# Kernel taps at half-step offsets, tap products for four channel groups in one matmul, all first loads in one ring, engine lists ordered anew

## The chip, the cores and the metric

The kernel runs on one core of one Trainium2 chip. The metric is the device time of one execution in microseconds (us). Each kernel is run several times. A run is called slow here when it is over 1.5% above the fastest run of the same kernel on that chip, otherwise fast. Ratios and comparisons below are of fast runs unless a sentence says otherwise; the median that is quoted first for a run is of all its runs, slow ones too. A profile is one further execution, seen by the hardware profiler; its span is 1.5 to 2.9 us shorter than that execution's measured time.

Engine names in the profile: PE is the matmul engine, PEld its weight loads, DVE the vector engine, ACT the scalar engine, POOL and SP two further queues.

## The reference

```python
def reference(A_u, ...):
    xn = _layernorm(A_u)                       # [1, 2048, 512]
    # branch A: S4 state space layer: a long convolution along the 2048 positions, by FFT
    logdA, dB = dt * A, dt * Bc                # 512 channels x 128 modes, complex
    P = jnp.exp(logdA[:, :, None] * l)         # l = 0..2047
    K = jnp.einsum("dn,dnl,dn->dl", Cc, P, dB).real
    s = irfft(rfft(pad(xn)) * rfft(pad(K)))[:2048] + xn * Dskip
    # branch B: the one row with the largest xn @ w_r goes through a gated expert (F = 1376)
    g = silu(xn + scatter(expert(xn[row])))
    return A_u + s * g
```

(Padding, casts and helper functions are left out.) The kernel does the convolution in the frequency domain: the spectrum of `xn` by two DFT passes (`f1`, `f2`), and the spectrum of the filter `K` by a trick: `K` is sampled at a few positions around 20 centres ("taps"), and a fixed matrix `W` turns these samples into the spectrum.

## The kernel before

Everything is recorded into a list of operations with their read and write footprints; a fixed list for each engine says in which order it issues them, and semaphores are set from the footprints. So nearly all matmuls have one source line (the helper's), and groups are told apart by the names of their tiles: `PB<-GG,QQ` are the tap products, `PB<-KT,CA` the transposes behind them, `PB<-KT,W` the filter's spectrum, `PB<-XN,CB` and `PB<-BT,F2T` the two DFT passes, `PB<-PAB,FA` the way back, `PB<-CA,AD` the arguments of the exponentials.

The part that changes most, the samples of `K`. Channels come in 4 quarters `q` of 128; each quarter is done in two chunks (`js`), 8 chunks in all. A chunk is 64 channels: 4 groups `gp` of 16 (`jj`). For every channel the product over the 128 modes of `QQ` (32 positions) and `GG` (20 centres), real and imaginary part (`ci`), is one 32-column matmul of 20 moving columns:

```python
def kgen(c):
    q, js = c // 2, c % 2
    qb = c % 2
    mms = []
    for jj in range(16):
        for ci in range(2):
            for gp in range(4):
                # out: 32 partitions of bank 4; weights 128 x 32; moving 128 x 20
                mms.append((PB[32*gp:32*gp+32, 4, 20*jj:20*jj+20], QQ[:, qb, ci, gp, 0:32, jj],
                            GG[:, 0, ci, :, 32*gp + 16*js + jj], ci == 0, ci == 1))
    kp = KP[:]
    # ... one more pair of matmuls for the sample at position 0 ...
    g.M(mms)                                   # 128 tap matmuls in one go
    act(KT[:, js], PB[:, 4, 0:320].rearrange("p (c t m) -> p m t c", t=5, m=4), ACT.Copy, 320)
    # ... 16 transposes: IDENT (32 columns) x KT[:, js, m, :, :], 80 contiguous columns ...
    act(KT2[:, q, :, 64*js:64*js+64]..., PB[:, 4, 0:320]..., ACT.Copy, 320)
```

`QQ` is laid out `[128, buffer, ci, gp, position, 16 jj]`: the weight columns of one channel are 16 elements (32 bytes) apart. `GG` is `[128, ci, centre, 128 channels]`: the 20 moving columns of one channel are 128 elements (256 bytes) apart. In both layouts the vector engine's operations write whole rows of channels.

The loads and the fillers:

```python
g.dma(SP, [(LD4[:], ...)]); pload("ar"); ca_load = g.dma(SP, [(CA[:], ...)]); ...  # parameters: SP's ring
for q in range(4):
    xl = g.dma(AC, [xsrc[q]])                                 # X in four parts: ACT's ring
# [...]
for k in range(4):                                            # warm-up: 16 matmuls of 128x512
    g.M([(PB[:, 6 + k % 2, :], AT[:, 0, 0:128], warm, True, True) for _ in range(4)])
# [...]
_FILL = [(7, 6, 5), (11, 2, 4), ..., (154, 2, 20)]            # place in PE's list, bank, number of fillers
```

The comments are ours. A ring is the DMA queue of the engine that issues the transfers. The fillers are dense matmuls into free banks (the profile has 47 on their own line, L275); they are meant to hold the matmul engine's clock up where it would wait. `spec(pt)` makes the spectrum in four parts, s0 to s3, each in four steps; a step is 40 matmuls `KT,W`, a copy by ACT, two multiplications by DVE, 32 matmuls `PAB,FA` and a copy by ACT.

## Time and profile before

| what | before |
|---|---|
| time, median of 3 runs | 209.75 us (209.18 to 210.92) |
| profiled span | 206.6 us |
| PE busy, matmuls | 175.7 us, 3170 |
| ACT busy / DVE busy | 136.2 / 142.6 us |
| first bn_stats / first normalized XN / first tap product | 8.8 / 27.7 / 59.1 us |
| second spectrum (s1) starts | 106.3 us |

(bn_stats is the vector engine's first step of the layer norm, XN the normalized input.)

From the page of before: busy time with the share of the span and the number of instructions; the span in 40 slices with tenths of busy time (PE) and of the full matmul clock (PEclk); the instruction queue with packets, MB and share; and the chain of work that ended last.

```profile
PE 175.7 (85%) x3170; PEld 127.9 (62%) x3181; DVE 142.6 (69%) x344; ACT 136.2 (66%) x164; POOL 13.9 (7%) x24
...
PE   6099998889993999967999998999999649999960
...
PEclk9999999995555589985999999889999757999997
...
q8 instruction: 25, 0.41, 0.8%
...
PE 60%; ACT 12%; DVE 10%; issue 8%; DMA 7%; SPq 0%; DVEq 0%
```

The matmul engine is busy nearly throughout, and 60% of the chain lies on it. "issue" is time in which an engine waited for nothing that the profile shows. The clock row is to be read with care at its start: the trace records the clock of before only from 29.8 us on, and the page draws the time before that as full, although 16 `CA,AD` matmuls that take 0.62 us at 100.9 took 1.04 us at 23.7. The groups of instructions of before, by cost: line, engine, operation, tiles, shapes, count | busy us, mean ns of one | idle time before them and what ended it.

```profile
L187 PE MATMUL PB<-KT,W 128*128 128x128 bf16 x640 | 40.1, 224 | 0.7 <-ACT KT L740 0.4
...
L740 ACT ACTIVATE KT<-PB 128x320 bf16<-128x320 f32 x16 | 10.7, 671 | 20.2 <-PE PB L187 20.2
L187 PE MATMUL PB<-GG,QQ 128*32 128x20 bf16 x1024 | 19.8, 223 | 3.9 <-issue 3.9
...
L187 PE MATMUL PB<-BT,F2T 128*64 128x256 bf16 x128 | 11.3, 307 | 1.9 <-issue 1.6
```

The mean of a matmul (223 ns) is its length in the pipeline, not its share of the time: 1024 of them took 19.8 us, 19 ns each. That is why throughput is better read from the timeline, in which successive matmuls of one kind are one row: start, length, what, and in brackets the idle time before it. Before, around the first and the fourth chunk of taps:

```profile
59.06 2.42 PE L187 MATMUL PB<-GG,QQ 128*32 128x20 bf16 x128
61.30 0.27 PE L187 MATMUL PB<-KP,CB 128*4 128x64 bf16 x2
61.49 0.58 PE L187 MATMUL PB<-FT,ERU 128*128 128x1 bf16 x14
65.19 0.75 PE L187 MATMUL PB<-FT,ERU 128*128 128x1 bf16 x19 [3.11 <-issue]
...
87.89 0.33 PE L187 MATMUL PB<-KT,CA 128*32 128x80 bf16 x16
...
91.34 2.25 PE L187 MATMUL PB<-GG,QQ 128*32 128x20 bf16 x118
94.79 0.39 PE L187 MATMUL PB<-GG,QQ 128*32 128x20 bf16 x10 [1.20 <-issue]
```

A chunk of taps takes 2.42 us. Inside runs of one kind of matmul there are five holes that no wait in the profile explains: 3.1 us (above, at 62.1), 1.6, 1.2 (above, at 93.6), 2.1 and 2.7 us, in sum 10.6 us. Counted over all of the trace's records of the matmul engine (matmuls, weight loads, semaphore instructions), they come after instructions 1212, 2235, 2490, 5305 and 5561: multiples of 256 apart, give or take one. The DMA records of the packed trace tie them to the instruction queue: a packet of 16,384 bytes lands in or just before each hole (at 63.6, 88.7, 93.6, 161.3 and 167.5 us), and the hole ends 1.2 to 1.6 us after that landing. (The other 20 packets land without such a hole.)

The table of windows gives, for a stretch of time, busy us and instruction count of PE, PEld, DVE, ACT, POOL, then mean matmul clock, DMA share and GB/s. The stretch from the first tap product to the second spectrum, before:

```profile
59.10:106.30 47.20, 40.71 (x1000) 32.83 (x1001) 26.55 (x61) 29.63 (x38) 3.09 (x5) 0.77 0.56 187
```

### The profile page before, as it was taken

The page shows a single profiled execution, that of the slowest core. Times are in us where ns is not written, and L with a number is a line of the kernel's source. Part 1 is how long each engine was busy: PE and PEld are TensorE (multiplying, and loading weights), DVE is VectorE, ACT ScalarE, POOL GpSimd, SP SyncE. Part 2 cuts the span into 40 slices and gives each one's busy share as a digit, 9 for nine tenths or more (in the row PEclk, how much of TensorE's full clock was granted, in tenths as well). Part 3 has the DMA queues.
Part 4 walks back from the last instruction along what each step waited for, and adds up shares of the span by engine and source line. Part 5 has one row for each costly group of instructions (what it writes and reads, how often), then busy time and mean ns, then how long its engine had stood idle before and what let it go on. Part 6 is the DMA issues. An engine that isn't in the chain of part 4 may idle for free.

```text
span 206.6 us, 7069 instructions
## 1 busy us (share of the span) xinstructions
PE 175.7 (85%) x3170; PEld 127.9 (62%) x3181; DVE 142.6 (69%) x344; ACT 136.2 (66%) x164; POOL 13.9 (7%) x24
## 2 busy tenths in 40 slices
PE   6099998889993999967999998999999649999960
PEld 2044547555883766946898875876799327895420
DVE  1599589997970789801699999959999205542634
ACT  2059589997703978661799999986688422566431
POOL 0074000000000203000000000200002400000000
PEclk9999999995555589985999999889999757999997
DMA  6989972225595692980037297441349852366874
GB/s 176 347 272 405 415 292 84 86 83 156 138 297 185 175 293 51 408 370 8 18 87 205 75 261 198 127 112 33 75 105 306 191 123 51 94 195 178 189 167 102
DMA packets 40528, 36.85 MB, mean 178 GB/s; under 512 B 26577, under 2 KB 35922, under 8 KB 39602
## 3 DMA queue, kind: packets, MB, share of 16 engines
q1 hardware_dynamic: 37458, 20.12, 35.7%
q0 software_dynamic: 2464, 14.19, 19.5%
q10 hardware_dynamic: 576, 2.10, 3.1%
q8 instruction: 25, 0.41, 0.8%
q14 instruction: 5, 0.04, 0.1%
HBM read 25.91 MB, written 10.49 MB: 176 GB/s over the span
## 4 chain that ended last, share of the span: by engine, by line
PE 60%; ACT 12%; DVE 10%; issue 8%; DMA 7%; SPq 0%; DVEq 0%
PE PB L187 58%; DMA STG<-in_A_A_re_dram 3%; ACT U L740 3%; DMA DD<-scr_z 3%; ACT K2T L740 2%; PE PB L275 2%; DVE TT L711 2%; DVE XN L720 2%; ACT QQ L740 2%; ACT ZT L740 1%; DMA scr_z<-ZT 1%; DVE ZB L711 1%; ACT KT L740 1%; ACT XN L740 1%; DVE T L711 1%
## 5 line engine op out<-in xcount | busy, mean ns | idle before, releaser
L187 PE MATMUL PB<-KT,W 128*128 128x128 bf16 x640 | 40.1, 224 | 0.7 <-ACT KT L740 0.4
L187 PEld LDWEIGHTS PB<-KT,W 128*128 128x128 bf16 x640 | 37.3, 100 | 4.2 <-ACT KT L740 1.6
L187 PE MATMUL PB<-CA,AD 32*128 32x256 bf16 (+1 forms) x192 | 24.9, 309 | 5.7 <-DVE AD L724 5.0
L711 DVE TENSOR_TENSOR TT<-GG,ZB 128x512 bf16<-128x512 bf16 (+2 forms) x64 | 27.7, 469 | 0.4
L711 DVE TENSOR_TENSOR PAB<-U,K2T 128x1024 bf16<-128x1024 bf16 x32 | 21.3, 685 | 8.6 <-ACT K2T L740 8.6
L740 ACT ACTIVATE K2T<-PB 128x1024 bf16<-128x1024 f32 x16 | 16.5, 1034 | 14.5 <-PE PB L187 14.4
L187 PEld LDWEIGHTS PB<-CA,AD 32*128 32x128 bf16 x192 | 15.5, 114 | 15.7 <-DVE AD L724 5.9
L711 DVE TENSOR_TENSOR QQ<-QQ,EE 128x2048 bf16<-128x2048 bf16 x16 | 19.5, 1220 | 7.1 <-ACT QQ L740 7.0
L740 ACT ACTIVATE KT<-PB 128x320 bf16<-128x320 f32 x16 | 10.7, 671 | 20.2 <-PE PB L187 20.2
L187 PE MATMUL PB<-GG,QQ 128*32 128x20 bf16 x1024 | 19.8, 223 | 3.9 <-issue 3.9
L187 PEld LDWEIGHTS PB<-GG,QQ 128*32 128x32 bf16 x1024 | 18.8, 170 | 6.3 <-issue 4.3
L187 PE MATMUL PB<-PAB,FA 64*128 64x128 bf16 x512 | 17.9, 222 | 0.6 <-ACT ZT L740 0.4
L740 ACT ACTIVATE U<-PB 128x1024 bf16<-128x1024 f32 x16 | 16.3, 1037 | 2.6 <-PE PB L187 2.6
L740 ACT ACTIVATE ZT<-PB 128x1024 bf16<-128x1024 f32 x16 | 16.5, 1033 | 2.0 <-PE PB L187 2.0
L740 ACT ACTIVATE EE<-PB 128x1024 bf16<-128x1024 f32 x16 | 15.5, 1029 | 2.2 <-PE PB L187 2.2
L187 PEld LDWEIGHTS PB<-PAB,FA 64*128 64x128 bf16 x512 | 15.1, 97 | 3.0 <-ACT ZT L740 0.8
L740 ACT ACTIVATE AT<-PB 128x1024 bf16<-128x1024 f32 x16 | 16.5, 1085 | 0.7 <-PE PB L187 0.7
L711 DVE TENSOR_TENSOR TF<-PB,XN 128x512 bf16<-128x512 f32 x12 | 8.1, 686 | 11.9 <-PE PB L187 8.3
L275 PE MATMUL PB<-CA 128*128 128x512 bf16 x47 | 15.1, 439 | 1.3 <-issue 1.2
L711 DVE TENSOR_TENSOR GG<-TT 128x512 bf16<-128x512 bf16 (+2 forms) x32 | 15.0, 469 | 0.4
L187 PE MATMUL PB<-XN,CB 128*128 128x256 bf16 (+1 forms) x80 | 14.4, 314 | 0.6 <-DVE XN L720 0.5
L187 PE MATMUL PB<-BT,F2T 128*64 128x256 bf16 x128 | 11.3, 307 | 1.9 <-issue 1.6
(131 smaller groups left out, 226.7 us busy)
## 6 DMA issues: line engine op xcount, KB each, us to landing
W<-c_w POOLq DMA_DIRECT2D x4, 1280.0 KB, 9.0
scr_a<-AT SPq DMA_DIRECT2D x8, 512.0 KB, 3.6
BT<-scr_a SPq DMA_DIRECT2D x8, 512.0 KB, 5.0
scr_z<-ZT SPq DMA_DIRECT2D x16, 256.0 KB, 3.4
DD<-scr_z SPq DMA_DIRECT2D x6, 512.0 KB, 5.0
X<-in_A_u_dram ACTq DMA_DIRECT2D x4, 512.0 KB, 7.0
XR<-in_A_u_dram POOLq DMA_DIRECT2D x4, 512.0 KB, 6.3
out_dram<-XR SPq DMA_DIRECT2D x8, 256.0 KB, 3.1
```

Of the source, the lines that this page charges most:

```text
L187: fns.append(lambda e, o=o, l=l, r=r, st=st, sp=sp, tp=tp: e.matmul(o, lhsT=l, rhs=r, start=st, stop=sp, tile_position=tp, skip_group_chec ...
L275: n.fns = [lambda e, o=o: e.matmul(o, lhsT=lhs, rhs=rhs, start=True, stop=True, tile_position=(0, 0), skip_group_check=True)] * k
L711: g.V(lambda e: e.tensor_tensor(out=o, in0=a, in1=b, op=op), [o], [a, b], n, mode)
L720: g.V(lambda e: e.tensor_scalar(out=o, in0=a, scalar1=s1, scalar2=s2, op0=op, op1=op2), [o], ins + ([s2] if not isinstance(s2, (int, float ...
L740: nd = g.A(lambda e: e.activation(out=o, in_=i, func=func, **kw), [o], ins, n + (110 if "bias" in kw else 0), after=[ph["pre"]] if tab els ...
```

## The change

The intent is to cut instructions on the matmul engine and holes in its stream, and to start earlier.

1. The positions of the taps move by half a step (plus and minus 0.5 to 15.5 in place of -16 to 15). `QQ` then has 32 rows instead of 33, so that 4 x 32 weight columns lie evenly spaced.
2. A matmul takes the weights of one channel of *each* of the four groups (128 columns, 32 bytes apart) and the moving columns of the same four channels (4 x 20). It computes all 16 combinations of group and group, of which 4 are used. 1024 matmuls become 256. The copy by ACT becomes three copies of 480, 400 and 400 columns instead of one of 320, and the transposes pick the useful blocks; there are 20 of them in a chunk instead of 16, and they now read and write with steps.
3. Fillers and warm-up go. X goes into the same ring as the parameters, its first part ahead.
4. All five lists are ordered anew (router and expert ahead of the power chain, `f1` between).

The core of the diff (lists, constants and the filler's bookkeeping cut):

```diff
-_FILL = [(7, 6, 5), (11, 2, 4), (12, 2, 5), ... (154, 2, 20)]
+_FILL = []
 _ORDER = { ... all five lists anew ... }
-    pos = list(range(-1, -17, -1)) + list(range(0, 16))
+    pos = [-(i + 0.5) for i in range(16)] + [i + 0.5 for i in range(16)]
-        QQ = place("QQ", [128, 2, 2, 4, 33, 16], BF16)
+        QQ = place("QQ", [128, 2, 2, 4, 32, 16], BF16)
-        KT = place("KT", [128, 2, 4, 5, 16], BF16)
+        KT = place("KT", [128, 16, 4, 20], BF16)
-        for q in range(4):
-            xl = g.dma(AC, [xsrc[q]])
+        for q in range(5):                      # parts of 2, 2, 4, 4, 4
+            xl = g.dma(SP, [xsrc[q]])
-        g.sec = "warm"                          # 16 warm-up matmuls
-        ...
         def kgen(c):
-            for jj in range(16):
-                for ci in range(2):
-                    for gp in range(4):
-                        mms.append((PB[32 * gp:32 * gp + 32, 4, 20 * jj:20 * jj + 20], QQ[:, qb, ci, gp, 0:32, jj],
-                                    GG[:, 0, ci, :, 32 * gp + 16 * js + jj], ci == 0, ci == 1))
+            j0 = 0
+            for nj, bank in ((6, 4), (5, 5), (5, 4)):
+                mms = []
+                for k in range(nj):
+                    jj = j0 + k
+                    for ci in range(2):
+                        mms.append((PB[:, bank, 80 * k:80 * k + 80], sap(QQ, 0, 128, 4096 * qb + 2048 * ci + jj, [[16, 128]]),
+                                    sap(GG, 0, 128, 2560 * ci + 16 * js + jj, [[32, 4], [128, 20]]), ci == 0, ci == 1))
+                g.M(mms)
+                act(KT[:, j0:j0 + nj].rearrange("p a b c -> p (a b c)"), PB[:, bank, 0:80 * nj], ACT.Copy, 80 * nj)
+                j0 += nj
             ...
-                    mms.append((PB[32 * m:32 * m + 32, 4, 80 * gp:80 * gp + 80], IDENT[:, 32 * gp:32 * gp + 32], KT[:, js, m, :, :], ...))
+                    for t0, nt, sel in (((0, 5, IDENT),) if m < 3 else ((0, 4, IDENT), (4, 1, IDZ))):
+                        mms.append((sap(PB, 32 * m, 32, 5 * 512 + 64 * t0 + gp, [[64, nt], [4, 16]]), sel[:, 32 * gp:32 * gp + 32],
+                                    sap(KT, 0, 128, 20 * gp + m + 4 * t0, [[4, nt], [80, 16]]), ...))
```

In `sap(tile, first partition, partitions, offset, [[step, count], ...])` steps count elements of 2 bytes.

## The prediction

> **What bounds it now (span 206.6 us).** The chain of waits is PE 60%, ACT 12%, DVE 10%, "issue" 8%. By stages (table of windows): 0-27.7 us, loads (DMA share 0.91), cold args and warm-up/filler matmuls, until the first normalized XN at 27.66; 27.7-59.1, DVE (29.4 of 31.4 us busy) until the first tap-product matmuls; 59.1-106.3, PE (40.8 of 47.2; DVE 26.6, ACT 29.6); 106.3-142.3, ACT (34.8 of 36.0) and PE (34.2); 142.3-190, PE (41.9 of 47.7); then the tail.
>
> The PE stages have five "issue" holes inside runs of one matmul kind: 3.1 (at 62.1), 1.6, 1.2, 2.1, 2.7 us: 10.6 us. In the trace they lie multiples of 256 PE instructions apart, and the instruction queue moved 25 packets of 16 KB. [...]
>
> **Removed, added, moved.**
> - Tap products: 1024 matmuls (32 columns, N=20; 8 x 2.42 us) become 256 (128 columns, N=80). KT,W pairs (128 columns, N=128) take 60 ns warm, 114 cold; estimate 45-75 ns a pair, 1.4-2.4 us a chunk. The strided 128-column load is unmeasured here[...]. Gain 3-6 us of PE.
> - PE matmuls fall from 3179 to 2374, and the dense blocks go: 7-9 of the 10.6 us of holes vanish (one may stay at the router/expert passes, 152 thin matmuls in a row).
> - Fillers and warm-up, 63 matmuls: on the chain about 4 us in 11.9-26; elsewhere in idle time.
> - ACT: KT evacuation (671 ns) becomes 480+400+400 columns (about 1.5 us); about +6 us of ACT in all, 2-3 us of it where ACT bounds.
> - Loads: first X piece leads one ring, so bn_stats starts near 4 us instead of 8.8 and A_re need not share with 1.5 MB of X; with no fillers in front of the exps, ACT finishes them near 18.5 instead of 25.8. First XN near 20-21: 6-7 us earlier.
> - Order: router and expert precede the power/GG chain. DVE has the same 47.8 us before the first taps, started 4 us earlier: first taps near 55 (4 us earlier), f1 and expert already done. To the second spectrum (106.3 before) PE has about 36 us of work, DVE about 34: near 91-94. The rest (100 us before) loses two fetch holes (4.8) and about 3 us of taps, gains 2-3 of ACT.
>
> **Sum.** Prologue/first taps -4, middle -9, second half -5 to -6: span about 187, measured about **190 us** (span is 3 us below the median). Range **181 to 200**. Faster by over 2%: 0.95; within: 0.04; slower: 0.01.
>
> **What would show it.** Holes over 1 us inside PE groups: none or one. Tap group at or under 2.4 us per chunk with x256. First XN near 20-21, first taps near 55. PE instructions about 2370. ACT busy about 142; DVE unchanged. Second spectrum's matmuls starting near 93.
>
> **What would make it wrong.** Strided 128-column loads not fast (over 100 ns a pair: +6 us PE); PE clock at half for longer without fillers; strided PSUM writes or strided moving reads slowing the transposes; one ring delivering X slower; ACT becoming the bound; fetch holes moving to other dense runs.

Two passages are cut where marked, because the traces do not show what they said of the hardware. Its stages (-4, -9, -5 to -6) come to -18 to -19 us, which from the span of 206.6 makes 187.6 to 188.6, put there as about 187 and, with 3 us for the span, as 190 measured. Its "dense blocks" are the chunks of 128 tap matmuls with their 128 weight loads: 256 instructions in 2.42 us, while the instruction packets of before land 3.3 us or more apart; that their supply was too slow for such a chunk was the author's reading. `A_re`, which was to share with less of X, took 6.4 us from issue to landing in before and 3.0 in after.

## The result

| | before | after |
|---|---|---|
| time, median of 4 runs in turn on one chip | 209.83 us (209.18 to 210.92) | 226.91 us (224.42 to 227.52) |
| ratio of mean times | | 1.079 (95%: 1.069 to 1.088) |
| profiled span | 206.6 us | 225.0 us |
| first bn_stats / first XN / first tap product | 8.8 / 27.7 / 59.1 | 3.7 / 21.3 / 60.5 |
| spectra s1, s2, s3 start | 106.3, 142.3, 172.3 | 112.0, 157.9, 191.3 |

Ratios here and below are the mean time of one kernel's fast runs over the mean of the other's fast runs in the same rounds, so they are not quite the ratio of the medians quoted. The change made the kernel 8% slower. The lines of the page of after that answer to those of before:

```profile
PE 190.3 (85%) x2377; PEld 144.6 (64%) x2378; DVE 144.0 (64%) x339; ACT 144.5 (64%) x186; POOL 14.2 (6%) x24
...
PE   0683887949999999999999789899999999996380
...
PEclk9999999955878579656999999755599996999766
...
q8 instruction: 18, 0.29, 0.5%
...
PE 52%; DVE 26%; ACT 10%; DMA 7%; issue 2%; SPq 2%; DVEq 0%
```

There are 793 matmuls fewer, and yet PE is busy 14.6 us longer. The instruction packets went from 25 to 18, and "issue" from 8% of the chain to 2%. The groups of after:

```profile
L187 PE MATMUL PB<-KT,W 128*128 128x128 bf16 x640 | 44.4, 231 | 0.6 <-ACT K2T L753 0.3
...
L187 PE MATMUL PB<-GG,QQ 128*128 128x80 bf16 x256 | 40.4, 327 | 1.0 <-ACT KT L753 0.7
...
L753 ACT ACTIVATE KT<-PB 128x400 bf16<-128x400 f32 (+2 forms) x32 | 15.7, 499 | 25.8 <-PE PB L187 25.8
...
L187 PE MATMUL PB<-BT,F2T 128*64 128x256 bf16 x128 | 14.6, 371 | 0.5 <-ACT K2T L753 0.5
```

The tap products doubled, from 19.8 to 40.4 us: 20.6 us, more than the whole loss. Two groups whose instructions are the same as before also grew, `KT,W` by 4.3 and `BT,F2T` by 3.3 us; they run in more half-clock stretches (digits 5 in the clock row; the mean recorded clock is 0.83 against 0.88). The timeline of after, first and second chunk (a chunk is 12 and 20 matmuls now, with another kind between):

```profile
60.45 1.96 PE L187 MATMUL PB<-GG,QQ 128*128 128x80 bf16 x12 [0.20 <-DVE GG L724]
...
63.07 3.10 PE L187 MATMUL PB<-GG,QQ 128*128 128x80 bf16 x20
66.10 1.06 PE L187 MATMUL PB<-BT,F2T 128*64 128x256 bf16 x8
67.09 0.32 PE L187 MATMUL PB<-KT,CA 128*32 128x80 bf16 x4
...
67.83 0.20 PE L187 MATMUL PB<-KV,CB 1*32 1x64 bf16 x1
...
70.63 3.14 PE L187 MATMUL PB<-GG,QQ 128*128 128x80 bf16 x20
```

A group of 20 takes 3.1 us, 155 ns a matmul with its weight load; from start to start, without the last one's way through the pipeline, it is 146 to 150 ns in every chunk. The one chunk that runs in one piece (at 88.99) takes 4.84 us; elsewhere the pieces of 12 and 20 take 1.95 to 1.98 and 3.10 to 3.14 us. That is the same where the recorded clock is full and where it is half: something that does not follow the clock holds it up. The transposes of a chunk went from 0.26 us (87.89 to 88.15 in before) to 0.74 us (67.09 to 67.83). The window from the first tap product to the second spectrum, after:

```profile
60.50:112.00 51.50, 50.97 (x578) 41.45 (x580) 27.05 (x55) 30.72 (x45) 0.94 (x2) 0.73 0.39 143
```

PE is busy for 51.0 of 51.5 us with 422 matmuls fewer than in the 47.2 us of before. The start was gained as intended (first XN at 21.3 instead of 27.7 us), but the first tap product came no earlier. DVE waits for PE about 8 us in all between the two, where it waited 1.5 in the same stage of before. In the view of waits, from the first XN to the first tap product in after, the largest is this line (what waited, for what, us in total, times, longest):

```profile
DVE RB L741 <- PE PB L187: 5.1, 1, 5.1
```

The router's step now stands ahead of the power chain in DVE's list, and DVE waits 5.1 us for a matmul there.

### The profile page after: what moved, and what is told of

The parts are those of the page before. It is cut to its first block, busy times and chain, and to the rows that moved or that the text cites. A ratio compares the mean times of both kernels' runs of the same rounds, so it can differ in the third digit from the quotient of the medians.

```text
span 225.0 us, 5484 instructions
## 1 busy us (share of the span) xinstructions
PE 190.3 (85%) x2377; PEld 144.6 (64%) x2378; DVE 144.0 (64%) x339; ACT 144.5 (64%) x186; POOL 14.2 (6%) x24
## 4 chain that ended last, share of the span: by engine, by line
PE 52%; DVE 26%; ACT 10%; DMA 7%; issue 2%; SPq 2%; DVEq 0%
PE PB L187 51%; DVE TT L724 6%; DVE PAB L724 4%; DMA X<-in_A_u_dram 3%; ACT K2T L753 3%; DVE GG L724 3%; ACT XT L956 3%; DVE T L724 2%; DMA DD<-scr_z 2%; DVE ST L801 2%; ACT AT L753 2%; SPq L210 2%; DMA scr_z<-ZT 1%; DVE TF L724 1%; DVE ZB L724 1%
## 5 line engine op out<-in xcount | busy, mean ns | idle before, releaser
L187 PE MATMUL PB<-KT,W 128*128 128x128 bf16 x640 | 44.4, 231 | 0.6 <-ACT K2T L753 0.3
L187 PEld LDWEIGHTS PB<-KT,W 128*128 128x128 bf16 x640 | 39.9, 104 | 4.8 <-ACT K2T L753 1.9
L187 PE MATMUL PB<-GG,QQ 128*128 128x80 bf16 x256 | 40.4, 327 | 1.0 <-ACT KT L753 0.7
L187 PEld LDWEIGHTS PB<-GG,QQ 128*128 128x128 bf16 x256 | 35.7, 147 | 3.5 <-ACT KT L753 1.8
L753 ACT ACTIVATE KT<-PB 128x400 bf16<-128x400 f32 (+2 forms) x32 | 15.7, 499 | 25.8 <-PE PB L187 25.8
L724 DVE TENSOR_TENSOR TT<-GG,ZB 128x512 bf16<-128x512 bf16 (+2 forms) x64 | 27.7, 470 | 0.7
L753 ACT ACTIVATE AT<-PB 128x1024 bf16<-128x1024 f32 x16 | 15.9, 1022 | 7.6 <-PE PB L187 6.4
L187 PE MATMUL PB<-XN,CB 128*128 128x256 bf16 (+1 forms) x80 | 14.6, 325 | 5.7 <-ACT AT L753 4.4
L187 PE MATMUL PB<-BT,F2T 128*64 128x256 bf16 x128 | 14.6, 371 | 0.5 <-ACT K2T L753 0.5
L187 PE MATMUL PB<-DD,CB 128*128 128x512 bf16 x32 | 11.0, 449 | 4.0 <-DVE KV L724 2.9
L187 PEld LDWEIGHTS PB<-XN,CB 128*128 128x128 bf16 (+1 forms) x80 | 7.5, 112 | 10.7 <-ACT AT L753 5.7
```

Of the source, the lines that this page charges most:

```text
L187: fns.append(lambda e, o=o, l=l, r=r, st=st, sp=sp, tp=tp: e.matmul(o, lhsT=l, rhs=r, start=st, stop=sp, tile_position=tp, skip_group_chec ...
L724: g.V(lambda e: e.tensor_tensor(out=o, in0=a, in1=b, op=op), [o], [a, b], n, mode)
L753: nd = g.A(lambda e: e.activation(out=o, in_=i, func=func, **kw), [o], ins, n + (110 if "bias" in kw else 0), after=[ph["pre"]] if tab els ...
```

## The experiments

The theory after the result: the tap products are slow because their *moving* operand is read with a step of 256 bytes. Rivals: the weights, with their step of 32 bytes; the width of 80 columns itself, three quarters of it waste; the new order with its clock stretches.

Fifteen runs were made. Those of one call share a chip and the runs of before: probe, a_mv, a_wt, a_grp; then fix, fix_tr, fix_tr_q, fix_xact; then b_few, b_nofill, fix_fill, fix_r5; then b_few_nf, fix_q2, fix_r3. Kernels of different calls are compared only by their ratios to before, or roughly. The medians of before in these were 207.6 to 209.1 us.

### probe: the disputed pair alone

This kernel is not a version of the other two and its output is wrong. It runs batches of 32 pairs of weight load and matmul, N = 80 (in two batches 20), with one access pattern each, and 8 dense matmuls of N = 512 after each batch. It was run once; the batches are compared within that run.

```python
TESTS = [ # name, weight step, weight columns, moving pattern
    ("pp", 1, 128, [[1, 80]]), ("wst", 16, 128, [[1, 80]]), ("mst", 1, 128, [[32, 4], [128, 20]]), ("both", 16, 128, ...),
    ...  # moving steps of 2, 4, 8, 16, 32 elements; runs of 4 or 20; 32-column forms
]
```

> Matmuls by themselves (the output is zeros on purpose, so wrong): 15 batches of 32 weight-load/matmul pairs on a warm array, 8 filler matmuls of N=512 between them; only the step between elements of the weights and of the moving operand differs. The changed kernel's taps took 155 ns a pair, warm or cold. Theory A (the moving operand is read with a step of 256 bytes, and that costs about 2 ns a column): packed/packed 35 to 60 ns a pair, strided weights alone the same, strided moving alone about 155, both about 155; four-column-group N=20 pairs about 19 ns strided. Theory B (the strided 128-column weight load is slow): strided weights alone about 155, strided moving alone 35 to 60. Theory C (neither; the taps wait for their evacuations and the clock): all four under 80 ns.

Timeline of the probe: start, length, what.

```profile
58.08 1.31 PE L94 MATMUL PB<-M_pp,W_pp 128*128 128x80 bf16 x32
59.22 1.89 PE L74 MATMUL PB<-FW 128*128 128x512 bf16 x8
60.95 2.13 PE L94 MATMUL PB<-M_wst,W_wst 128*128 128x80 bf16 x32
62.91 1.90 PE L74 MATMUL PB<-FW 128*128 128x512 bf16 x8
64.64 4.57 PE L94 MATMUL PB<-M_mst,W_mst 128*128 128x80 bf16 x32
69.03 3.23 PE L74 MATMUL PB<-FW 128*128 128x512 bf16 x8
72.10 4.81 PE L94 MATMUL PB<-M_both,W_both 128*128 128x80 bf16 x32
...
80.11 2.20 PE L94 MATMUL PB<-M_m,W_m 128*128 128x80 bf16 x32
82.16 1.89 PE L74 MATMUL PB<-FW 128*128 128x512 bf16 x8
83.88 2.55 PE L94 MATMUL PB<-M_m,W_m 128*128 128x80 bf16 x32
86.25 1.91 PE L74 MATMUL PB<-FW 128*128 128x512 bf16 x8
...
109.30 1.32 PE L94 MATMUL PB<-M_run,W_run 128*128 128x80 bf16 x32
```

From the start of a batch to the start of the next row, divided by 32, one pair takes:

| weights | moving operand | ns a pair |
|---|---|---|
| packed | packed | 36 |
| step 32 B | packed | 61 |
| packed | step 4 B (at half clock) / 8 B | 64 / 74 |
| packed | step 16 B / 32 B / 64 B | 143 / 146 / 137 |
| packed | as in the change (256 B) | 137 |
| step 32 B | as in the change | 145 |
| packed | runs of 4 elements (8 B), 256 B apart | 36 |
| packed | runs of 20 elements | 36 |
| 32 columns, step 32 B | N = 20, step 256 B (as in before) | 23 |
| 32 columns, packed | N = 20, packed | 9 |
| 32 columns, packed | N = 80, the transposes' pattern (160 B) | 43 |
| 32 columns, packed | N = 80, packed | 13 |

The batch with a step of 4 bytes (the first `M_m` row, at 80.11) fell into a stretch of half clock, which the trace records until 82.0 us: its pairs are 67 ns apart there and 40 ns in the last two, when the clock is full again. So at full clock that step costs about 4 ns, and not 28. The batch with 8 bytes ran at full clock.

The moving operand's step is what costs: 36 to 137 ns. The weights' step alone costs 25 ns, and 8 ns on top of the other. The width of 80 is cheap (36 ns). From a step of 16 bytes on, the cost is flat (1.7 to 1.8 ns a column), and runs of four elements (8 bytes) side by side make it vanish. Below that it depends on the step: 40 ns at 4 bytes and full clock, 74 at 8 bytes. Why the steps cost what they do, the probe does not show.

A second thing shows in the fillers: 8 dense matmuls take 1.9 us, but 3.2 us after mst, 3.6 after both, 3.4 and 2.9 after the steps of 16 and 32 bytes. In each of these four batches the recorded clock fell to half, 3.1 to 4.3 us after its start (at 68.35, 75.18, 92.24 and 99.07 us), although the timeline shows no wait of the matmul engine there. In the batch with the step of 64 bytes, which was as long (4.5 us, from 103.2), it did not fall, and the fillers after it took 1.9 us. So slow reads went with a lowered clock in four of five such batches; what decides it was not shown.

### a_mv and a_wt: one operand packed in the changed kernel

Both read other data than they should, so their output is wrong; everything else is the kernel after.

```diff
 # a_mv
-sap(GG, 0, 128, 2560 * ci + 16 * js + jj, [[32, 4], [128, 20]])
+sap(GG, 0, 128, 2560 * ci + 80 * (16 * js + jj), [[1, 80]])
 # a_wt
-sap(QQ, 0, 128, 4096 * qb + 2048 * ci + jj, [[16, 128]])
+sap(QQ, 0, 128, 4096 * qb + 2048 * ci + 128 * jj, [[1, 128]])
```

> The changed kernel, but the tap matmuls read their moving operand packed (wrong numbers on purpose; same count, sizes and order). Theory A: a group of 32 falls from 4.95 us to 1.3 to 2.4, the PE clock stays full for longer, and the span falls by 20 to 28 us, to about 200 us measured. Theory B: the group and the span stay within 3 us of the changed kernel's 226.9. Theory C: within 5 us.

> The changed kernel, but the tap matmuls load their weights packed (wrong numbers on purpose). Theory A: the group of 32 stays at 4.9 to 5.1 us, the time within 3 us of 226.9. Theory B: group 1.3 to 2.4 us, time about 200. Theory C: within 5 us of 226.9.

a_mv took 193.5 and 196.1 us in its fast runs (198.3 and 198.7 in two slow ones), where the fast runs of before took 204.8 and 206.3. a_wt took 221.7 us in its one run. By the two fast runs each, a_mv is at 0.948 of before. Against the 226.9 us of the change, on another chip, packing the moving operand takes off some 30 us, and packing the weights about 5 (within 3 were expected). The line of the tap products in the groups of a_mv:

```profile
L187 PE MATMUL PB<-GG,QQ 128*128 128x80 bf16 x256 | 19.0, 234 | 0.8 <-ACT KT L753 0.7
```

A chunk in one piece is 2.39 us, in a_wt 4.56 us; from start to start the median pair of each chunk is 62 to 63 ns, in a_wt 138. Both agree with the probe: 61 ns for strided weights alone, 137 for the strided moving operand alone. In a_mv the recorded clock is full without a break from 59.6 to 179.1 us, and `KT,W` is back at 40.2 and `BT,F2T` at 10.0 us. So the half-clock stretches of after in that time belong to the slow tap products and not to the missing fillers.

### a_grp: the old tap matmuls in the new kernel

The four 32-column matmuls of before, everything else new; the result is right. One thing follows along: ACT copies only the 20 useful columns of each channel, and its group of `KT` copies takes 9.3 us instead of 15.7.

```diff
-    mms.append((PB[:, bank, 80*k:80*k+80], sap(QQ, ..., [[16, 128]]), sap(GG, ..., [[32, 4], [128, 20]]), ...))
+    for gp in range(4):
+        mms.append((PB[32*gp:32*gp+32, bank, 20*k:20*k+20], QQ[:, qb, ci, gp, 0:32, jj],
+                    GG[:, 0, ci, :, 32*gp + 16*js + jj], ci == 0, ci == 1))
```

> The changed kernel with the old form of the tap products (128 matmuls a chunk, 32 columns, N=20, four column groups), all else as changed; the result is right. Theories A and B: taps back to about 2.4 us a chunk, some instruction-fetch holes back (up to 5 us in all), measured time 200 to 208 us. Theory C (order and evacuations are to blame): within 5 us of 226.9.

Its one fast run took 205.6 us; three slow ones 208.7 to 213.7, and so there is no ratio. The profile is of the fast run: chunks of 2.41 us, 24 instruction packets (before has 25), and 2.1 us of "issue" among the tap products. Undoing this form takes about 21 us off the change (one fast run, on another chip). In the fast run the rest of the change gains nothing over the fast runs of before (204.8 and 206.3), but the spread leaves that weak.

### fix: the moving operand in runs of four, with the right result

`GG` is a product of powers, and the channel order within it is set where its arguments are written. If the four groups lie innermost, the four channels of one matmul are neighbours. Only addresses change:

```diff
 # powers' arguments, and the B and C factors, are written with the four groups innermost
-o = sap(PB, 0, 128, 512 * (2 * pair + h) + 32 * gp, [[128, 4], [1, 32]])
+o = sap(PB, 0, 128, 512 * (2 * pair + h) + gp, [[128, 4], [4, 32]])
-o = sap(PB, 0, 128, 512 * (4 + ip // 2) + 256 * (ip % 2) + 32 * qq, [[128, 2], [1, 32]])
+o = sap(PB, 0, 128, 512 * (4 + ip // 2) + 256 * (ip % 2) + qq, [[128, 2], [4, 32]])
 # tap products
-sap(GG, 0, 128, 2560 * ci + 16 * js + jj, [[32, 4], [128, 20]])
+sap(GG, 0, 128, 2560 * ci + 64 * js + 4 * jj, [[128, 20], [1, 4]])
 # ... and the transposes, the last tap and the skip term pick accordingly
```

> The changed kernel with one layout turned: the channels of a block of 128 are stored with the four groups innermost, so a tap matmul reads its moving operand in runs of four elements instead of a step of 256 bytes; counts, sizes and engine lists as in the changed kernel, right result. Theory A (the moving step is the cause): tap pair 60 to 75 ns, PE clock full from about 60 us on, measured 193 to 198 us, as with the wrong-on-purpose packed operand; faster than before by 4 to 8%. If that gain came from the wrong numbers and not from the access: above 215 us.

It took 199.4 us (197.6 to 199.6, 4 fast runs), ratio to before 0.954 (0.945 to 0.964). The result is right. Its groups, timeline and windows:

```profile
L187 PE MATMUL PB<-GG,QQ 128*128 128x80 bf16 x256 | 19.3, 239 | 1.6 <-DVE GG L724 0.7
```

```profile
61.04 0.95 PE L187 MATMUL PB<-GG,QQ 128*128 128x80 bf16 x12
...
62.65 1.44 PE L187 MATMUL PB<-GG,QQ 128*128 128x80 bf16 x20
...
64.69 0.32 PE L187 MATMUL PB<-KT,CA 128*32 128x80 bf16 x4
```

```profile
61.00:99.00 38.00, 36.62 (x578) 29.84 (x578) 27.66 (x56) 30.68 (x45) 1.09 (x2) 0.96 0.52 189
```

The 20 tap products take 1.44 us instead of 3.10. From the first tap product to the second spectrum it is 38.0 us instead of 51.5, with the same 578 matmuls and the clock at 0.96 instead of 0.73. This one pattern was the difference between 8% slower and 5% faster. In before, the clock of the same stage was 0.77 (the window above), so part of the lead over before is clock too.

What most likely limits the pair now can be read from the traces, but was not tried: from start to start it is 62 to 63 ns (the median) in most chunks, as in a_mv and as in the probe's batch with strided weights and a packed moving operand (61). Packed weights as well gave 36 ns there; an estimate from these two is 256 x 26 ns, or 6 to 7 us of the matmul engine. No run here packs both in the kernel.

The edit has a price in another place. The arguments are now written to PSUM with a step of 16 bytes, and 16 of those matmuls take 1.89 us where the same 16 take 1.04 in after. In the timeline of fix:

```profile
21.13 1.89 PE L187 MATMUL PB<-CA,AD 32*128 32x128 bf16 x16
```

That is 118 against 65 ns a matmul, and in the second half's powers, at the recorded full clock in both, 1.05 us against 0.62 for the same 16. The first tap product came at 61.0 us (60.5 in after), so at most half a microsecond of it is seen there.

### fix_tr: the transposes' read packed too

The transposes still read `KT` with a step of 160 bytes. This version lets ACT write `KT` transposed, so that they read contiguously.

```diff
-act(KT[:, j0:j0+nj].rearrange("p a b c -> p (a b c)"), PB[:, bank, 0:80*nj], ACT.Copy, 80*nj)
+act(sap(KT, 0, 128, j0, [[16, 80], [1, nj]]), PB[:, bank, 0:80*nj].rearrange("p (k c) -> p c k", c=80), ACT.Copy, 80*nj)
-sap(KT, 0, 128, gp + 4*m + 16*t0, [[16, nt], [80, 16]])
+sap(KT, 0, 128, 16*(gp + 4*m + 16*t0), [[256, nt], [1, 16]])
```

> As fix, and the evacuation writes the tap products transposed, so the 16 to 20 sorting matmuls of a chunk read runs of 16 instead of a step of 160 bytes (right result). Theory A: their group falls from about 0.75 us to 0.25-0.35, in all 3 to 4 us of PE; the evacuations may take longer because of short runs of writes (568 ns for 480 columns now), and then ACT eats it. Expected measured time 1 to 4 us below fix; if evacuations are over 750 ns, equal or slower.

The time was 200.9 us, fast runs 199.7 and 197.2, ratio 0.952 (0.937 to 0.968), the same as fix. Its profile is of a slow run. The transposes of a chunk went from 0.73 to 0.43 us in seven of the eight chunks, some 2 us in all, but ACT's copies grew from a mean of 501 to 572 ns, 2.5 us in all. So the same cause was at work in the transposes, and its removal does not show in the time.

### fix_tr_q: work for DVE ahead of the router

The wait of 5.1 us in DVE's list was the suspect for the late first tap product. Seven operations of the power chain go ahead of the router's.

```diff
 "vector": [..., 131,
+    133, 135, 134, 136, 138, 137, 139,
     192, 193, 194, 196, ...]
```

> As fix_tr, and on DVE seven operations of the power chain go ahead of the router's first copy, where DVE idles 5.1 us in the changed kernel. If the router put ahead of the power chain is what made the first taps come at 60.5 us instead of my 55: first taps 3 to 5 us earlier and the time 2 to 5 us below fix_tr. If the first taps wait for something else, no change within 1 us.

It took 200.1 us, ratio 0.960 (0.953 to 0.967), and its first tap product came at 61.7 us: missed. DVE's single long wait became four shorter ones (1.8, 1.2, 2.2 and 1.9 us) in the router's steps: with the small ones DVE waited 7.8 us for PE, where it had been 8.2 in fix_tr. The wait was spread and not removed. PE's list then waited 2.9 us for ACT's copies of `f1`, and ran at about half speed: eight `CA,AD` matmuls took 1.88 us at 53.6 and the expert's eleven down matmuls 3.7 us at 57.2, where before, at the recorded full clock, took 1.04 (at 75.7) and 2.54 (at 77.7).

### fix_xact: X back on its own ring

```diff
-xl = g.dma(SP, [xsrc[q]])
+xl = g.dma(AC, [xsrc[q]])     # and first in ACT's list
```

> As fix, but X is loaded again from the ACT ring beside the parameters on the SP ring. If the one ring with X's first piece ahead gives the early start: bn_stats begin near 7-9 us instead of 3.7, first XN 2 to 5 us later than in fix (about 21.3), time 1 to 5 us above fix. If the absence of fillers gives it: first XN within 1 us, time within 1 us of fix.

198.7 us, ratio 0.955 (0.945 to 0.966): the same as fix. The first bn_stats came at 4.2 us (3.7 in fix), the first XN at 20.3 us, if anything earlier (21.2). So the early start does not come from sharing one ring. The expectation took such a result as a sign that the missing fillers give it; b_nofill below shows that these account for 2.7 of the 6.4 us of the first XN, and hardly for bn_stats (7.9 us there). What is left is the order of the loads, X's first part ahead, together with the new lists; no run takes the two apart.

### b_few: what the instruction holes are worth

In the kernel *before*, one matmul of 128 columns and N = 20 in place of four of 32 columns: as few instructions as in the change, without its slow read of 80. The output is wrong.

```diff
-    for gp in range(4):
-        mms.append((PB[32*gp:32*gp+32, 4, 20*jj:20*jj+20], QQ[:, qb, ci, gp, 0:32, jj],
-                    GG[:, 0, ci, :, 32*gp + 16*js + jj], ci == 0, ci == 1))
+    mms.append((PB[:, 4, 20*jj:20*jj+20], sap(QQ, 0, 128, 4224*qb + 2112*ci + jj, [[16, 128]]),
+                GG[:, 0, ci, :, 32*(jj % 4) + 16*js + jj], ci == 0, ci == 1))
```

> The kernel before, with the four 32-column tap matmuls of each step made one of 128 columns and N=20 (wrong numbers on purpose): 768 matmuls and as many weight loads fewer, all else and the engine lists as before. If the instruction-fetch holes are real and on the critical path (my reading of before): the five holes of 10.6 us go to one or none, instruction packets 25 to about 19, and the time falls by 8 to 14 us, of which the shorter tap groups (1.4 to 2.2 us instead of 2.42) explain at most 5. If the holes only moved waiting that would have been there anyway: at most 5 us.

195.2 us (194.3 to 195.4), ratio 0.943 (0.934 to 0.952). The groups and the page's instruction queue of b_few:

```profile
L187 PE MATMUL PB<-GG,QQ 128*128 128x20 bf16 x256 | 17.7, 218 | 0.0
```

```profile
q8 instruction: 19, 0.31, 0.6%
```

A chunk of taps takes 2.2 us instead of 2.42, so at most 2 us come from the matmuls themselves. (Its pair is 64 ns, about that of fix with four times the columns, which fits the strided weights as the limit.) There is no hole over 0.9 us from 10 to 184 us, and the packets are 19 instead of 25. Some 10 of the 12 us, then, go with the holes: 768 matmuls fewer, each with its weight load, and the stream of instructions keeps up. This part of the reasoning behind the change is right and large.

### b_nofill: before without fillers

```diff
-_FILL = [(7, 6, 5), ... (154, 2, 20)]
+_FILL = []
-g.M([(PB[:, 6 + k % 2, :], AT[:, 0, 0:128], warm, True, True) for _ in range(4)])
+g.M([(PB[:, 6 + k % 2, 0:1], AT[:, 0, 0:128], warm[:, 0:1], True, True)])
```

> The kernel before without its 47 filler matmuls and with the 16 warm-up matmuls cut to 4 of N=1; right result. My prediction said the fillers sat on the chain for about 4 us in 11.9 to 26: then first XN comes 2 to 4 us before 27.7 and the time falls by 2 to 4 us. Rival: the fillers hold the clock, and without them the half-clock stretches grow and the time rises by 1 to 5 us.

202.1 us, ratio 0.979 (0.969 to 0.989), about 4.4 us. The first XN came 2.7 us earlier (25.0). Two of the holes of before are still there (2.4 us at 60.9, 1.0 at 152.1); in sum the holes over 1 us fell from 10.6 to 3.5 us. So this run removes holes as well as fillers, and the 4.4 us cannot be put down to the fillers' own time alone.

### b_few_nf: both

> The kernel before with both cuts at once, 768 fewer tap matmuls (wrong numbers on purpose) and no fillers, old engine lists. If the two gains add (5.75% and 2.1% alone): 0.915 to 0.93 of before, 3 to 6 us under the corrected kernel's 0.952, and then the new lists with their added evacuations cost that much. If the new lists are themselves worth something: not below 0.945.

The edit is that of b_few and of b_nofill together; the output is wrong. 197.4 us, fast runs 196.9 to 197.7, ratio 0.955 (0.947 to 0.964). The two gains do not add up: with both it is no faster than b_few alone. A likely reason is that they share the holes: b_few removes all five, b_nofill some 7 of their 10.6 us, and a hole can be removed only once. And the old lists with few instructions and no fillers are as fast as fix with the new lists, so the new order of lists and loads, together with the larger copies and transposes that the right result needs, brings nothing that shows beside these.

### fix_fill and fix_q2: the late first tap product

fix_fill puts 8 fillers ahead of the second half of `f1`, meant to hold the clock up (`_FILL = [(48, 4, 8)]`). fix_q2 interleaves the router's and the powers' operations on DVE and puts three `f1` groups behind the first taps on PE.

> As fix, with 8 filler matmuls of N=512 in the 2.7 us in which PE waits for an AT buffer (46.7 to 49.4). If half clock from 42 to 59 delays the first taps: the clock is full again by about 53, first taps near 57 to 59 and the time 1 to 4 us below fix. If the DVE chain, which ends at about 60.4, sets the first taps: they stay at 60 to 61 and the time within 1.5 us of fix.

> The corrected kernel with the power and GG work put between the router's hops on DVE (as the old list had it), and three of the six f1 groups of the second half after the first taps on PE and ACT; right result. If the router in a block (8 us of DVE idle) and the f1 groups ahead hold the first taps: first taps at 54 to 58 us instead of 60.4 to 61, time 2 to 5 us below fix (0.93 to 0.945 of before). If something else holds them: unchanged within 1 us.

fix_fill took 200.2 us, ratio 0.968 (0.954 to 0.982). Its clock was full from 59.6 to 179 us, but the first tap product came at 62.0, waiting for DVE's `GG`. fix_q2 took 202.6 us; only one of its four runs was fast (198.0), its profile is of a slow run, and its first tap product came at 62.1. Both missed. DVE's list, PE's list and the clock share this stretch, and to relieve any one of them alone moved nothing. A fourth limit shows in both profiles: the expert's eleven down matmuls, which the new order puts ahead of the first taps (at 56 us; 77.7 in before), waited 1.6 and 1.7 us for the load of their weights (`PE PB <- DMA WD`). Which of them would have to go together stays open.

### fix_r5 and fix_r3: fix again

The same kernel as fix, as a yardstick.

> The corrected kernel again, on the chip of these runs, for the comparison with the others of this call: 0.945 to 0.965 of before, tap pair near 72 ns, no hole over 1 us inside a matmul group from the first taps to the last.

> The corrected kernel once more as the yardstick on this chip: 0.945 to 0.96 of before.

197.0 us, ratio 0.952 (0.944 to 0.960), and 200.1 us, ratio 0.961 (0.945 to 0.977). On three chips the repaired change is 4 to 5% faster than before. It is the version with the right result that beats both kernels.

## Why the prediction was wrong

The step that failed is the term for the tap products, in the words of the prediction: "estimate 45-75 ns a pair (...) 1.4-2.4 us a chunk. (...) Gain 3-6 us of PE." It was 155 ns a pair (146 to 150 from start to start) and 4.84 us a chunk in one piece, 2.42 more than before; over the eight chunks, the groups show 40.4 us instead of 19.8, a loss of 20.6 us. The term had the cost of the pair wrong, because it left out the read of the moving operand.

- **Where the estimate came from.** It took the time of the `KT,W` pairs (128 columns, N = 128, 60 ns), whose moving operand is contiguous, and worried only about the weights' step. Under "what would make it wrong" strided moving reads stand beside the transposes, not beside the taps. The diff shows the pattern `[[32, 4], [128, 20]]`, and the probe shows that exactly it takes 137 of the 145 ns.
- **Why the old kernel hid it.** The old matmuls read with the same step of 256 bytes. They stream as many columns in a chunk (128 x 20 = 2560, as now 32 x 80), yet took 0.95 ns a column against 1.89 now. They work on four separate column groups of the array, which the new one occupies at once, and the matmuls of the four groups start together. The probe's trace shows it: in the batch with the transposes' pattern, 32 columns and N = 80, the four matmuls of the four groups start within 6 to 11 ns, and the next four 155 to 160 ns later (133 after the first four). So four strided reads together take hardly longer than one in the wide form (137). In before, too, the taps start in fours, the first fours within 10 ns, and a chunk's fours are 69 ns apart on average.
- **What the packed form would have been worth.** Even with the moving operand packed, a chunk is 2.39 us (a_mv; fix has 2.55 with a wait in it) against 2.42, most likely because the weights are still read with a step. The gain of the wide matmul as written is not in the matmuls, of which three quarters are waste, but in the instructions that are saved. So the estimate of 45-75 ns a pair comes out then (62 to 63), but "Gain 3-6 us" would still have been wrong by a few us.
- **The rest of the loss.** The transposes lost 0.48 us in each chunk, nearly 4 us; fix_tr shows that 0.30 of it is the same cause, and the rest (four more matmuls, writes with a step) was not taken apart. The clock is the second effect: with the slow batches it averaged 0.73 in the stage after the first taps, without them 0.96 (fix) and 1.00 (a_mv), and `KT,W` and `BT,F2T` grew by 7.6 us in sum over the trace. Against before, with 0.77 in its own such stage, the clock is only a little lower. The prediction had named half clock as a danger, but as one of missing fillers.

What was right:

- **The holes.** "7-9 of the 10.6 us of holes vanish": no hole of this kind is left in PE's waits of after, the packets fell from 25 to 18, and b_few shows that it is worth about 10 us in the kernel before.
- **The start.** First bn_stats at 3.7 us ("near 4"), first XN at 21.3 ("20-21"). The reasons given were right in part: the missing fillers give 2.7 us of the first XN (b_nofill), and the one ring gives nothing (fix_xact).
- **The fillers.** "About 4 us": b_nofill gained 4.4. That it is the same number is partly luck, since the first XN came only 2.7 us earlier and the holes, which the prediction counts elsewhere, shrank by 7 us in that run.
- **ACT and DVE.** 144.5 us (about 142 predicted) and 144.0 (unchanged, 142.6). PE had 2377 matmuls (about 2370).
- **The middle.** From the first taps to the second spectrum 36 to 39 us were predicted (55 to 91-94); with the packed read it is 38.0 us in fix and 36.2 in a_mv.

What was wrong besides:

- **First taps near 55 us.** They came at 60.5, and at 60 to 62 in every version with the new lists. The prediction took DVE's 47.8 us of work and 4 us of earlier start. It left out that the router, put ahead, makes DVE wait for PE, 5.1 us at once and 8 in all (1.5 in before). Three attempts to mend it failed, so how much belongs to which is open.
- **That the gains add up.** b_few_nf shows that fewer instructions (12 us) and no fillers (4 us) together give about 9. The predicted sum of 20 us was not reached with a packed read either; fix gave 8 to 10.

## What to carry to other kernels

Before merging small matmuls into wide ones, look at the step of the *moving* operand, not only at the shapes: here a pair of N = 80 took 36 ns packed and 137 to 146 ns with each element 16 or more bytes from the last, and four neighbours in a run restored it by a mere reordering of channels. Look at the weights' step as well (61 ns instead of 36). Take a duration from the trace as an estimate only for an instruction with the same access pattern, and a duration from a probe only together with the clock that was recorded while it ran. Fewer instructions were worth far more (about 10 us) than the matmul time that they carried, and gains measured alone need not add up.
